# Attention followed by a Mish MLP on one core: casting loads and TensorE transposes for the first two batches, and units of work spread anew

## The chip, the cores and the metric

One NeuronCore of a Trainium2 chip runs the whole program. The metric is device time in microseconds (us) of one execution, as the median of several (tail_first_b has one run); a profile of one execution comes with it.

## The reference, cut to what matters

```python
q, k, v: (8 batches, 12 heads, 448 rows, 64) fp32
scores = q @ k.T / 8 ;  e = exp(scores - m)
attn   = e / (sum(e) + exp(-m))            # "softmax off by one"
x      = (attn @ v), heads side by side    # 3584 x 768
h      = x @ w_in                          # 768 -> 2048
g      = h * tanh(softplus(h))             # Mish
out    = g @ w_out                         # 2048 -> 768, fp32
```

The kernel leaves out m (the inputs are small), so the denominator is sum(e) + 1.

## The kernel before: the parts that matter

The program is a hand-written order of **slots**. Slot j (0 to 47) does the attention scores of head pair j; six slots make a batch, two slots make a **group** of four heads. At every even slot the sums and the product with v (attend) of the group before are done. Between them, TensorE gets **units** of the MLP of earlier batches: `mm1` (six matmuls of 448 columns, x by w_in, evicted by VectorE into `h_sb`) and `mm2` (eight matmuls of 384 columns, Mish(h) by w_out; two units make one output tile). Mish itself runs on ScalarE, which also does all exps; its table is exchanged before and after (1.28 us each time in the trace).

```python
    def load(j, names="kqv"):                      # fp32, 229 KB each, sync queue
        ...
            nc.sync.dma_start(out=st, in_=src[b, h0 : h0 + 2].rearrange("h (p t) d -> p h (t d)", t=NT))

    def do_cast(j, eng):                           # to bf16, on VectorE or Pool
        mb = half.tile([P, 2, NT, 2, D], BF16, tag="mb", name="mb")
        for i, name in enumerate("kq"):
            eng.tensor_copy(...)
        if j >= NPAIR:                             # batch 1 and later: DMA transpose
            qk = qk_pool.tile([128, 2, S], BF16, tag="qk", name="qk")
            nc.sync.dma_start_transpose(...)
            qk_t[j] = qk
        else:                                      # batch 0: TensorE, in transposes(j)
            cast[j] = mb

    def mish(b):
        ...
        for i in range(4):
            f = slice(i * n, (i + 1) * n)
            nc.scalar.activation(out=gm[:, f, :], in_=h_sb[:, f, 0:MAIN], func=AF.Mish)
        nc.scalar.activation(out=gt[:, :, o : o + TAIL], in_=h_sb[:, :, MAIN:S], func=AF.Mish)
        nc.scalar.preload_act_table_set("natural_log_exp_and_others")

        def slot(j, units, late=False):
            ...                                    # casts for j + 2, loads for j + 4
            scores(j, 0)
            take(1)                                # one unit
            if j + 1 < J: transposes(j + 1)
            if g is not None: sums(g)
            take(1)
            scores(j, 1)
            take((rest + 1) // 2)
            if g is not None: attend(g, 0); attend(g, 1)
            take(len(units), last=True)

        for p in range(B):
            m1 = mm1_units(p - 1) if p >= 1 else []
            m2 = mm2_units(p - 2) if p >= 2 else []   # 12 for even batches, 16 for odd ones
            for i in range(NPAIR):
                ...   # i = 0: four of m2; i = 1..4: four of m1 each; i = 5: what is left of m2
                if i == 4 and p >= 1:
                    mish(p - 1)                       # then eight of m2 at once
```

Of PSUM, the memory that matmuls write to, the kernel gives four banks to scores, two to attend, and two (pool `m`) to sums, transposes, `mm1` and `mm2` together.

The softmax here doesn't subtract the row's maximum and nothing guards it: scores larger than these inputs give would overflow.

Of the kernel before, what the change touches and what calls it, by code (L numbers as in the profile page):

```python
# [9 lines left out]
BF16 = mybir.dt.bfloat16  # L10
# [5 lines left out]
def kernel(  # L16
# [14 lines left out]
    nc = tc.nc  # L31

    B, H, S, D = q.shape
    d_model, d_ff = moe_w_in.shape
    NPAIR = H // 2
    J = B * NPAIR
    NT = 4
# [7 lines left out]
    FF_T = d_ff // 128  # L45
    HALF = d_model // 2
    SCALE = 1.0 / float(D) ** 0.5
    AHEAD = 4

    singles = ctx.enter_context(tc.tile_pool(name="singles", bufs=1))  # L50
    stage = ctx.enter_context(tc.tile_pool(name="stage", bufs=AHEAD - 1))
    half = ctx.enter_context(tc.tile_pool(name="half", bufs=3))
    v_pool = ctx.enter_context(tc.tile_pool(name="v", bufs=6))
    qk_pool = ctx.enter_context(tc.tile_pool(name="qk", bufs=4))
    e_pool = ctx.enter_context(tc.tile_pool(name="e", bufs=3))
    work = ctx.enter_context(tc.tile_pool(name="work", bufs=2))
# [9 lines left out]
    w_out_sb = singles.tile([128, FF_T, d_model], BF16, name="w_out_sb")  # L66
    h_sb = singles.tile([128, FF_T, S], FP32, name="h_sb")

    loaded, cast, qk_t, v_t, e_t, x_t = {}, {}, {}, {}, {}, {}
    rc_t, gm_t, gt_t = {}, {}, {}  # L70

    def load(j, names="kqv"):
        b, h0 = j // NPAIR, 2 * (j % NPAIR)
        for name in names:
            src = {"q": q, "k": k, "v": v}[name]
            st = stage.tile([P, 2, NT * D], FP32, tag=name, name=f"{name}_f")
            nc.sync.dma_start(  # L77
                out=st, in_=src[b, h0 : h0 + 2].rearrange("h (p t) d -> p h (t d)", t=NT)
            )
            loaded[j, name] = st  # L80

    def do_cast(j, eng):

        mb = half.tile([P, 2, NT, 2, D], BF16, tag="mb", name="mb")
        for i, name in enumerate("kq"):
            eng.tensor_copy(  # L86
                out=mb[:, i].rearrange("p t h d -> p h t d"),
                in_=loaded.pop((j, name)).rearrange("p h (t d) -> p h t d", d=D),
            )
        if j >= NPAIR:  # L90
            qk = qk_pool.tile([128, 2, S], BF16, tag="qk", name="qk")
            nc.sync.dma_start_transpose(
                out=qk.rearrange("c i (t p) -> c (i t) p", p=P),
                in_=mb.rearrange("p i t h d -> p (i t h d)"),
            )
            qk_t[j] = qk
        else:
            cast[j] = mb

    def cast_v(j):  # L100
        vb = v_pool.tile([P, 2, NT, D], BF16, tag="v", name="v_b")
        nc.gpsimd.tensor_copy(out=vb.rearrange("p h t d -> p h (t d)"), in_=loaded.pop((j, "v")))  # L102
        v_t[j] = vb

    def transposes(j):
        if j >= NPAIR:
            return
        mb = cast.pop(j)
        ps = m_pool.tile([128, 2, S], BF16, tag="m", name="tr_ps")
        for i in range(2):  # L110
            for t in range(NT):
                nc.tensor.transpose(
                    ps[:, i, t * P : (t + 1) * P],
                    mb[:, i, t].rearrange("p h d -> p (h d)"),
                    ident[0:P, 0:P],
                )
        qk = qk_pool.tile([128, 2, S], BF16, tag="qk", name="qk")
        nc.vector.tensor_copy(out=qk, in_=ps)
        qk_t[j] = qk
# [22 lines left out]
    def side_by_side(ps, g, weights):  # L142

        for t in range(NT):
            for c in range(4):
                nc.tensor.matmul(  # L146
                    ps[c * 32 : c * 32 + 32, 0:S],
                    lhsT=weights(2 * g + c // 2, c % 2, t),
                    rhs=e_t[2 * g + c // 2][:, t, c % 2, :],
                    start=(t == 0),  # L150
                    stop=(t == NT - 1),
                )

    def sums(g):
        den = m_pool.tile([128, 512], FP32, tag="m", name="den_ps")
        side_by_side(den, g, lambda j, h, t: ones[0:P, :])
        rc = work.tile([128, S], FP32, tag="rc", name="rc")
        nc.scalar.activation(out=rc, in_=den[:, 0:S], func=AF.Ln, bias=1.0)  # L158
        nc.scalar.activation(out=rc, in_=rc, func=AF.Exp, scale=-1.0)  # L159
        rc_t[g] = rc  # L160

    def attend(g, s):
        b, gi = divmod(g, GRP)
        if gi == 0 and s == 0:
            x_t[b] = work.tile([128, GRP, 2, S], BF16, tag="xT", name="xT")
        av = x_pool.tile([128, 512], FP32, tag="x", name="av_ps")
        side_by_side(
            av, g, lambda j, h, t: v_t[j][:, h, t, :].rearrange("p (d s) -> p s d", s=2)[:, s, :]
        )
        nc.vector.tensor_mul(x_t[b][:, gi, s, :], av[:, 0:S], rc_t[g])  # L170
        if s == 1:
            for j in (2 * g, 2 * g + 1):
                e_t.pop(j), v_t.pop(j)
            rc_t.pop(g)

    def mm1(b, ff, direct):
# [73 lines left out]
    def mm2_units(b):  # L250
        return [
            lambda t=t, n=n, part=part: mm2(b, t, n, part)
            for t in range(NC + b % 2)
            for n in range(2)
            for part in range(2)
        ]

    with tc.manual_schedule():
        nc.scalar.preload_act_table_set("natural_log_exp_and_others")
        load(0)  # L260
        load(1)
        load(2)
        make_identity(nc, ident)
        do_cast(0, nc.vector)
        cast_v(0)
        transposes(0)
        load(3)
        do_cast(1, nc.vector)
        cast_v(1)

        def load_w_in(i):
            c = slice(i * d_ff // 4, (i + 1) * d_ff // 4)
            for s in range(2):
                nc.gpsimd.dma_start(
                    out=w_in_sb[:, :, s, c],
                    in_=moe_w_in[:, c].rearrange("(g p s) f -> s p g f", p=128, s=2)[s],
                )

        def load_w_out(i):
            n = FF_T // 4  # L280
            nc.gpsimd.dma_start(
                out=w_out_sb[:, i * n : (i + 1) * n, :],
                in_=moe_w_out[i * n * 128 : (i + 1) * n * 128, :].rearrange(
                    "(f p) c -> p f c", p=128
                ),
            )

        def slot(j, units, late=False):




            def take(n, last=False):
                if late and not last:
                    return
                for _ in range(min(n, len(units))):
                    units.pop(0)()

            g = j // 2 - 1 if j % 2 == 0 and j >= 2 else None
            if j + 2 < J:  # L300
                do_cast(j + 2, nc.vector if j + 2 < NPAIR else nc.gpsimd)
                cast_v(j + 2)
            if j + AHEAD < J:
                load(j + AHEAD)
            if j <= 3:
                load_w_in(j)
            if 5 <= j <= 8:
                load_w_out(j - 5)
            rest = max(0, len(units) - 2)
            if j < J:  # L310
                scores(j, 0)
            take(1)
            if j + 1 < J:
                transposes(j + 1)
            if g is not None:
                sums(g)
            take(1)
            if j < J:
                scores(j, 1)
            take((rest + 1) // 2)  # L320
            if g is not None:
                attend(g, 0)
                attend(g, 1)
            take(len(units), last=True)

        for p in range(B):
            m1 = mm1_units(p - 1) if p >= 1 else []
            m2 = mm2_units(p - 2) if p >= 2 else []
            for i in range(NPAIR):
                late = p == 1 and i == 0  # L330
                if late:
                    units, m1 = m1[:2], m1[2:]
                elif i == 0:
                    units, m2 = m2[:4], m2[4:]
                elif i < 5:
                    units, m1 = m1[:4], m1[4:]
                else:
                    units, m2 = m2, []
                slot(p * NPAIR + i, units, late)
                if i == 4 and p >= 1:  # L340
                    mish(p - 1)
                    first, m2 = m2[:8], m2[8:]
                    for u in first:
                        u()
        m2 = mm2_units(B - 2)
        slot(J, m2[:4])
        m2 = m2[4:]
        m1 = mm1_units(B - 1, direct=True)
        while m1 or m2:
            if m1:  # L350
                m1.pop(0)()
            if m2 and len(m2) >= len(m1):
                m2.pop(0)()
        for u in mm2_units(B - 1):
            u()


# [28 lines left out]
```

## Time and profile before

| | before |
|---|---|
| median time | 479.41 us (3 runs, 479.09 to 489.27) |
| profiled execution | span 476.4 us, mean granted clock 0.965 |
| TensorE (PE) busy | 434.7 us, 91% |
| 16 DMA engines, 0 to 83 us | 8 or 9 tenths busy |

First, lines of the profile page's picture of the span in 40 slices of 11.9 us each. A digit is the busy share in tenths; PEclk is the granted TensorE clock in tenths. PE is TensorE, ACT ScalarE, DVE VectorE, POOL the engine GpSimd (Pool in the text), and L129 is line 129 of the kernel.

```profile
PE   3967697399998999999998999999998999999995
ACT  3873257935776559455766659455765658343200
PEclk9987799589999999999999999999999999999998
DMA  8999999419217860569117950579117600210222
```

From the ninth slice on PE is nearly full: mostly its work counts there. In the first eight slices PE is often not full, the clock dips, and DMA is at 8 or 9 in all but the last of them. So there are two stages with different limits, and one mean over the span would hide that.

Second, the chain of work that ended last, from its start (start us, us, what):

```profile
4.18 6.41 DMA q_f<-in_q_dram
10.65 7.00 DMA k_f<-in_k_dram
17.72 11.94 DMA v_f<-in_v_dram
29.66 22.01 DMA qk<-mb
...
52.71 4.47 PE h_ps L179 x12
...
57.70 2.38 PE h_ps L179 x12
...
81.63 5.60 ACT gm L207 x4
```

The start hangs on loads and on one DMA transpose that took 22 us to land. Twelve matmuls of `mm1` take 4.47 us right after that wait, and the next twelve 2.38 us, five us later.

Third, the waits of PE in the timeline (start us, us, engine, line, what; in brackets the idle time before, and what ended it):

```profile
36.76 0.99 PE L129 MATMUL s_ps<-qk 64*112 64x448 bf16 x4 [3.64 <-DMA qk<-mb]
51.71 0.99 PE L129 MATMUL s_ps<-qk 64*112 64x448 bf16 x4 [5.94 <-DMA qk<-mb]
90.45 0.62 PE L129 MATMUL s_ps<-qk 64*112 64x448 bf16 x2 [9.57 <-ACT e L136]
```

The last one is Mish of batch 0: ScalarE is busy with it from 80.3 to 89.5 us, and TensorE's next scores need an exp to free their PSUM buffer.

Fourth, from the steady part, again the chain of waits:

```profile
143.55 3.35 ACT e L136 x4
...
249.86 3.35 ACT e L136 x4
...
356.18 3.35 ACT e L136 x4
```

Once in two batches the slot after Mish has no units left, and PE waits for exps.

### The profile page before, as it was taken

What the parts mean: (1) busy time and instruction counts of PE and PEld (TensorE: products, weight loads), DVE (VectorE), ACT (ScalarE), POOL (GpSimd) and SP (SyncE); (2) the same over time, 40 slices, a digit from 0 to 9 for tenths busy, and PEclk for the clock granted to TensorE, in tenths of its full rate; (3) what the DMA queues carried; (4) which work ended last, traced back from release to release, by engine and by line L of the source; (5) the groups of instructions that cost most, each with busy time, mean ns of one, the idle gap of its engine ahead of it and who ended that gap; (6) DMA issues with size and microseconds to landing.
All of it is one profiled execution on the core that took longest, in us unless ns stands there. A gap on an engine that the chain in (4) does not pass through costs nothing.

```text
span 476.4 us, 7816 instructions
## 1 busy us (share of the span) xinstructions
PE 434.7 (91%) x3248; PEld 205.3 (43%) x3248; DVE 140.6 (30%) x235; ACT 266.9 (56%) x323; POOL 90.6 (19%) x150
## 2 busy tenths in 40 slices
PE   3967697399998999999998999999998999999995
PEld 1422243144453445544453445544453445555563
DVE  3512143024321343134421343134421343110021
ACT  3873257935776559455766659455765658343200
POOL 1722234203102140024103230114103100000000
PEclk9987799589999999999999999999999999999998
DMA  8999999419217860569117950579117600210222
GB/s 220 252 217 202 201 222 247 131 34 240 70 34 187 170 174 0 144 156 258 41 35 189 220 124 8 141 168 239 44 35 187 150 1 27 61 48 1 66 67 67
DMA packets 83364, 60.48 MB, mean 127 GB/s; under 512 B 42368, under 2 KB 79744, under 8 KB 83328
## 3 DMA queue, kind: packets, MB, share of 16 engines
q1 hardware_dynamic: 78016, 53.69, 48.1%
q0 software_dynamic: 5312, 6.29, 8.0%
q8 instruction: 25, 0.41, 0.4%
q14 instruction: 11, 0.09, 0.1%
HBM read 45.61 MB, written 11.01 MB: 119 GB/s over the span
## 4 chain that ended last, share of the span: by engine, by line
PE 83%; DMA 10%; ACT 5%; SPq 1%; issue 0%; DVE 0%
PE h_ps L179 32%; PE o_ps L231 32%; PE s_ps L129 8%; PE av_ps L146 7%; DMA qk<-mb 5%; PE den_ps L146 4%; ACT e L136 3%; DMA v_f<-in_v_dram 3%; DMA k_f<-in_k_dram 1%; DMA q_f<-in_q_dram 1%; ACT gm L207 1%; SPq L77 1%; ACT L209 0%; ACT L207 0%; ACT gt L208 0%
## 5 line engine op out<-in xcount | busy, mean ns | idle before, releaser
L136 ACT ACTIVATE e<-s_ps 112x896 bf16<-112x896 f32 x192 | 164.2, 916 | 137.2 <-PE s_ps L129 137.1
L179 PE MATMUL h_ps<-xT,w_in_sb 128*128 128x448 bf16 x768 | 163.3, 357 | 0.0
L231 PE MATMUL o_ps<-w_out_sb,gm 128*128 128x384 bf16 x768 | 133.3, 328 | 0.0
L179 PEld LDWEIGHTS <-w_in_sb 128*128 128x128 bf16 x768 | 68.9, 98 | 85.5 <-issue 31.9
L187 DVE COPY h_sb<-h_ps 128x448 f32<-128x448 f32 x112 | 70.0, 625 | 114.9 <-PE h_ps L179 114.9
L231 PEld LDWEIGHTS <-gm 128*128 128x128 bf16 x768 | 73.4, 98 | 57.0 <-issue 10.3
L129 PE MATMUL s_ps<-qk 64*112 64x448 bf16 x384 | 64.0, 398 | 31.5 <-ACT e L136 19.5
L239 DVE COPY o_sb<-o_ps 128x384 f32<-128x384 f32 x56 | 31.2, 558 | 162.9 <-PE o_ps L231 155.6
L86 POOL CAST mb<-k_f 112x512 bf16<-112x512 f32 x42 | 25.9, 617 | 184.3 <-DMA k_f<-in_k_dram 159.7
L129 PEld LDWEIGHTS <-qk 64*112 64x112 bf16 x384 | 20.2, 131 | 70.1 <-issue 55.8
L102 POOL CAST v_b<-v_f 112x512 bf16<-112x512 f32 x48 | 29.6, 616 | 88.0 <-PE av_ps L146 62.6
L146 PE MATMUL av_ps<-e,v_b 112*32 112x448 bf16 x768 | 42.9, 367 | 0.0
L170 DVE TENSOR_TENSOR xT<-av_ps,rc 128x448 bf16<-128x448 f32 x48 | 30.0, 625 | 40.3 <-PE av_ps L146 38.3
L207 ACT ACTIVATE gm<-h_sb 128x1536 bf16<-128x1536 f32 x28 | 39.2, 1471 | 0.1
L86 POOL CAST mb<-q_f 112x512 bf16<-112x512 f32 x42 | 25.9, 616 | 13.6 <-DMA q_f<-in_q_dram 13.0
L146 PEld LDWEIGHTS <-v_b 112*32 112x32 bf16 x768 | 18.9, 99 | 22.3 <-issue 9.1
L158 ACT ACTIVATE rc<-den_ps 128x448 f32<-128x448 f32 x24 | 13.1, 544 | 22.5 <-PE den_ps L146 22.5
L146 PE MATMUL den_ps<-e,ones 112*32 112x448 bf16 x384 | 25.3, 388 | 0.0
L231 PE MATMUL o_ps<-w_out_sb,gt 128*128 128x384 bf16 x128 | 22.0, 326 | 0.0
L191 ACT ACTIVATE gm<-h_ps 128x384 bf16<-128x384 f32 x16 | 7.9, 491 | 22.7 <-PE h_ps L179 22.7
L231 PEld LDWEIGHTS <-gt 128*128 128x128 bf16 x128 | 12.0, 98 | 9.5 <-issue 2.0
L159 ACT ACTIVATE rc<-rc 128x448 f32<-128x448 f32 x24 | 13.8, 576 | 0.8
(21 smaller groups left out, 68.6 us busy)
## 6 DMA issues: line engine op xcount, KB each, us to landing
k_f<-in_k_dram SPq DMA_DIRECT2D x48, 224.0 KB, 4.1
q_f<-in_q_dram SPq DMA_DIRECT2D x48, 224.0 KB, 4.3
v_f<-in_v_dram SPq DMA_DIRECT2D x48, 224.0 KB, 4.5
w_in_sb<-in_moe_w_in_dram POOLq DMA_DIRECT2D x8, 384.0 KB, 16.1
w_out_sb<-in_moe_w_out_dram POOLq DMA_DIRECT2D x4, 768.0 KB, 12.8
out_dram<-o_sb SPq DMA_DIRECT2D x8, 336.0 KB, 3.1
out_dram<-o_sb SPq DMA_DIRECT2D x8, 288.0 KB, 2.7
out_dram<-o_sb SPq DMA_DIRECT2D x8, 240.0 KB, 2.6
```

The source lines that it names most:

```text
L86: eng.tensor_copy(out=mb[:, i].rearrange("p t h d -> p h t d"), in_=loaded.pop((j, name)).rearrange("p h (t d) -> p h t d", d=D),)
L102: nc.gpsimd.tensor_copy(out=vb.rearrange("p h t d -> p h (t d)"), in_=loaded.pop((j, "v")))
L129: nc.tensor.matmul(sp[0:P, h, 0:S], lhsT=qk[r, 0, t * P : (t + 1) * P], rhs=qk[r, 1, :], start=True, stop=True,)
L136: nc.scalar.activation(out=e_t[j][:, t], in_=sp[0:P, :, 0:S], func=AF.Exp, scale=SCALE)
L146: nc.tensor.matmul(ps[c * 32 : c * 32 + 32, 0:S], lhsT=weights(2 * g + c // 2, c % 2, t), rhs=e_t[2 * g + c // 2][:, t, c % 2, :], start=( ...
L159: nc.scalar.activation(out=rc, in_=rc, func=AF.Exp, scale=-1.0)
L170: nc.vector.tensor_mul(x_t[b][:, gi, s, :], av[:, 0:S], rc_t[g])
L179: nc.tensor.matmul(hp[:, 0:S], lhsT=w_in_sb[:, dm // 2, dm % 2, ff * 128 : (ff + 1) * 128], rhs=x_t[b][:, dm // 2, dm % 2, :], start=(dm = ...
L187: nc.vector.tensor_copy(out=h_sb[:, ff, :], in_=hp[:, 0:S])
L207: nc.scalar.activation(out=gm[:, f, :], in_=h_sb[:, f, 0:MAIN], func=AF.Mish)
L231: nc.tensor.matmul(op[:, 0:HALF], lhsT=lhs, rhs=w_out_sb[:, ff, n * HALF : (n + 1) * HALF], start=(ff == 0), stop=(ff == FF_T - 1),)
L239: nc.vector.tensor_copy(out=o_sb[:, n * HALF : (n + 1) * HALF], in_=op[:, 0:HALF])
```

## The change

Its intent: bring q, k and v of batches 0 and 1 in as bf16 straight away, by DMAs that cast (issued by Pool, one ring, fixed order, w_in in between); transpose them on TensorE, so that no DMA transpose runs among the first loads; fetch w_out behind them; run Mish of batch 0 one slot later, where units of batch 1 can run beside it; and spread the units so that the slot after Mish always has some. The core of the diff, with cuts:

```diff
-    AHEAD = 4
+    SW = 2 * NPAIR
+    def load_cast(g, names="kqv", pairs=((0, 4),)):
+        kq, vb = group_tiles(g)
+        ...
+                nc.gpsimd.dma_start(out=dst, in_=rows_of(src, b, 4 * gi + h, n))
     def transposes(j):
-        if j >= NPAIR:
+        if j >= SW:
             return
+                for h in range(2):          # two half-width transposes in place of one
+                    nc.tensor.transpose(ps[h * D : h * D + D, i, t * P : (t + 1) * P], kq[:, i, o + h, t], ident[0:P, 0:P])
+    fetch = {
+        0: [lambda: load_w_in(3)],
+        3: [lambda: load_cast(3), lambda: load_w_out(0)],
+        5: [lambda: load_cast(4), lambda: load_w_out(1)],
+        7: [lambda: load_cast(5), lambda: load_w_out(2), lambda: load_w_out(3)],
+    }
+    def slot(j, units, pre=0, mish_of=None):
+        ...                                 # fetch, casts for j + 2 and loads for j + 4 from slot 12 on
+        run(units, pre)
+        if g is not None: sums(g)
+        if mish_of is not None: mish(mish_of)
+        scores(j, 0)
+        if g is not None: attend(g, 0); attend(g, 1)
+        run(units, (len(units) + 1) // 2)
+        if j + 1 < J: transposes(j + 1)
+        scores(j, 1)
+        run(units)
     with tc.manual_schedule():
+        load_cast(0, "kq", ((0, 2),))
+        load_cast(0, "v")
+        load_cast(0, "kq", ((2, 2),))
+        load_cast(1, "kq")
+        load_w_in(0)
+        load_cast(1, "v")
+        load_w_in(1)
+        load_cast(2)
+        load_w_in(2)
         ...
+                elif p == 1:
+                    slot(j, cut(m1, (2, 3, 3, 3, 3, 2)[i]))
+                elif p == 2:
+                    if i == 0:
+                        slot(j, cut(m1, 6), mish_of=0)
+                    elif i < 5:
+                        slot(j, [m1.pop(0)] + cut(m2, 1) + cut(m1, 2 if i < 3 else 1), pre=1)
+                    else:
+                        slot(j, m2, pre=1)
+                elif i == 0:
+                    slot(j, cut(m2, len(m2) - 10 + p % 2 * -2), pre=1)
+                elif i < 5:
+                    slot(j, cut(m1, 4), pre=1)
+                else:
+                    slot(j, m2, pre=1)
+                if i == 4 and p >= 2:
+                    mish(p - 1)
+                    run(cut(m2, len(m2) * 2 // 3))
```

From slot 12 on (batch 2 and later) loads, Pool casts and DMA transposes stay as they were.

More of the change, by code (lines that the diff above doesn't have):

```diff
@@ L47 @@
     SCALE = 1.0 / float(D) ** 0.5
-    AHEAD = 4
+    SW = 2 * NPAIR
     singles = ctx.enter_context(tc.tile_pool(name="singles", bufs=1))
-    stage = ctx.enter_context(tc.tile_pool(name="stage", bufs=AHEAD - 1))
+    stage = ctx.enter_context(tc.tile_pool(name="stage", bufs=3))
     half = ctx.enter_context(tc.tile_pool(name="half", bufs=3))
-    v_pool = ctx.enter_context(tc.tile_pool(name="v", bufs=6))
+    v_pool = ctx.enter_context(tc.tile_pool(name="v", bufs=3))
     qk_pool = ctx.enter_context(tc.tile_pool(name="qk", bufs=4))
@@ L67, with rows_of, group_tiles, load @@
     h_sb = singles.tile([128, FF_T, S], FP32, name="h_sb")
-    loaded, cast, qk_t, v_t, e_t, x_t = {}, {}, {}, {}, {}, {}
+    loaded, kq_t, qk_t, v_t, e_t, x_t = {}, {}, {}, {}, {}, {}
     rc_t, gm_t, gt_t = {}, {}, {}
-    def load(j, names="kqv"):
+    def rows_of(src, b, h0, n):
+        return src[b, h0 : h0 + n].rearrange("h (p t) d -> p h (t d)", t=NT)
+    def group_tiles(g):
+        if g not in kq_t:
+            kq_t[g] = half.tile([P, 4, 2, NT * D], BF16, tag="kq", name="kq")
+            v_t[g] = v_pool.tile([P, 4, NT * D], BF16, tag="v", name="v_b")
+        return kq_t[g], v_t[g]
+    def load_cast(g, names="kqv", pairs=((0, 4),)):
+        kq, vb = group_tiles(g)
+        b, gi = divmod(g, GRP)
+        for h, n in pairs:
+            for name in names:
+                if name == "v":
+                    dst, src = vb[:, h : h + n], v
+                else:
+                    i = "kq".index(name)
+                    dst = kq.rearrange("p (i hh) two c -> p i (hh two) c", i=2)[:, i, h : h + n]
+                    src = (k, q)[i]
+                nc.gpsimd.dma_start(out=dst, in_=rows_of(src, b, 4 * gi + h, n))
+    def load(j):
         b, h0 = j // NPAIR, 2 * (j % NPAIR)
-        for name in names:
-            src = {"q": q, "k": k, "v": v}[name]
+        for name, src in (("k", k), ("q", q), ("v", v)):
             st = stage.tile([P, 2, NT * D], FP32, tag=name, name=f"{name}_f")
-            nc.sync.dma_start(
-                out=st, in_=src[b, h0 : h0 + 2].rearrange("h (p t) d -> p h (t d)", t=NT)
-            )
+            nc.sync.dma_start(out=st, in_=rows_of(src, b, h0, 2))
             loaded[j, name] = st
-    def do_cast(j, eng):
-        mb = half.tile([P, 2, NT, 2, D], BF16, tag="mb", name="mb")
+    def do_cast(j):
+        kq, vb = group_tiles(j // 2)
+        o = 2 * (j % 2)
+        mb = kq[:, o : o + 2].rearrange("p i hh (t h d) -> p i (hh t) h d", h=2, d=D)
         for i, name in enumerate("kq"):
-            eng.tensor_copy(
+            nc.gpsimd.tensor_copy(
                 out=mb[:, i].rearrange("p t h d -> p h t d"),
@@ L89, in do_cast @@
             )
-        if j >= NPAIR:
-            qk = qk_pool.tile([128, 2, S], BF16, tag="qk", name="qk")
-            nc.sync.dma_start_transpose(
-                out=qk.rearrange("c i (t p) -> c (i t) p", p=P),
-                in_=mb.rearrange("p i t h d -> p (i t h d)"),
-            )
-            qk_t[j] = qk
-        else:
-            cast[j] = mb
-    def cast_v(j):
-        vb = v_pool.tile([P, 2, NT, D], BF16, tag="v", name="v_b")
-        nc.gpsimd.tensor_copy(out=vb.rearrange("p h t d -> p h (t d)"), in_=loaded.pop((j, "v")))
-        v_t[j] = vb
+        nc.gpsimd.tensor_copy(out=vb[:, o : o + 2], in_=loaded.pop((j, "v")))
+        qk = qk_pool.tile([128, 2, S], BF16, tag="qk", name="qk")
+        nc.sync.dma_start_transpose(
+            out=qk.rearrange("c i (t p) -> c (i t) p", p=P),
+            in_=mb.rearrange("p i t h d -> p (i t h d)"),
+        )
+        qk_t[j] = qk
     def transposes(j):
-        if j >= NPAIR:
+        if j >= SW:
             return
-        mb = cast.pop(j)
+        o = 2 * (j % 2)
+        kq = kq_t[j // 2].rearrange("p (i hh) two (t d) -> p i (hh two) t d", i=2, d=D)
         ps = m_pool.tile([128, 2, S], BF16, tag="m", name="tr_ps")
@@ L111, in transposes @@
             for t in range(NT):
-                nc.tensor.transpose(
-                    ps[:, i, t * P : (t + 1) * P],
-                    mb[:, i, t].rearrange("p h d -> p (h d)"),
-                    ident[0:P, 0:P],
-                )
+                for h in range(2):
+                    nc.tensor.transpose(
+                        ps[h * D : h * D + D, i, t * P : (t + 1) * P],
+                        kq[:, i, o + h, t],
+                        ident[0:P, 0:P],
+                    )
         qk = qk_pool.tile([128, 2, S], BF16, tag="qk", name="qk")
@@ L147, in side_by_side @@
                     ps[c * 32 : c * 32 + 32, 0:S],
-                    lhsT=weights(2 * g + c // 2, c % 2, t),
+                    lhsT=weights(c, t),
                     rhs=e_t[2 * g + c // 2][:, t, c % 2, :],
@@ L155, in sums @@
         den = m_pool.tile([128, 512], FP32, tag="m", name="den_ps")
-        side_by_side(den, g, lambda j, h, t: ones[0:P, :])
+        side_by_side(den, g, lambda c, t: ones[0:P, :])
         rc = work.tile([128, S], FP32, tag="rc", name="rc")
@@ L167, in attend @@
         side_by_side(
-            av, g, lambda j, h, t: v_t[j][:, h, t, :].rearrange("p (d s) -> p s d", s=2)[:, s, :]
+            av,
+            g,
+            lambda c, t: v_t[g].rearrange("p c (t d s) -> p c t s d", s=2, d=D // 2)[:, c, t, s],
         )
@@ L171, in attend @@
         if s == 1:
-            for j in (2 * g, 2 * g + 1):
-                e_t.pop(j), v_t.pop(j)
+            e_t.pop(2 * g), e_t.pop(2 * g + 1), v_t.pop(g)
             rc_t.pop(g)
@@ L256, in mm2_units, with load_w_in, load_w_out @@
         ]
+    def load_w_in(i):
+        c = slice(i * d_ff // 4, (i + 1) * d_ff // 4)
+        for s in range(2):
+            nc.gpsimd.dma_start(
+                out=w_in_sb[:, :, s, c],
+                in_=moe_w_in[:, c].rearrange("(g p s) f -> s p g f", p=128, s=2)[s],
+            )
+    def load_w_out(i):
+        n = FF_T // 4
+        nc.gpsimd.dma_start(
+            out=w_out_sb[:, i * n : (i + 1) * n, :],
+            in_=moe_w_out[i * n * 128 : (i + 1) * n * 128, :].rearrange("(f p) c -> p f c", p=128),
+        )
@@ new lines, with run @@
+    fetch = {
[4 more added lines that the diff above has]
+    }
+    def run(units, n=None):
+        for _ in range(len(units) if n is None else min(n, len(units))):
+            units.pop(0)()
+    def slot(j, units, pre=0, mish_of=None):
+        for f in fetch.get(j, ()):
+            f()
+        if SW <= j + 2 < J:
+            do_cast(j + 2)
+        if SW <= j + 4 < J:
+            load(j + 4)
+        run(units, pre)
+        g = j // 2 - 1 if j % 2 == 0 and j >= 2 else None
+        if g is not None:
+            sums(g)
+        if mish_of is not None:
+            mish(mish_of)
+        if j < J:
+            scores(j, 0)
+        if g is not None:
+            attend(g, 0)
+            attend(g, 1)
+        run(units, (len(units) + 1) // 2)
+        if j + 1 < J:
+            transposes(j + 1)
+        if j < J:
+            scores(j, 1)
+        run(units)
@@ L258, with cut @@
+    def cut(m, n):
+        part = m[:n]
+        del m[:n]
+        return part
     with tc.manual_schedule():
         nc.scalar.preload_act_table_set("natural_log_exp_and_others")
-        load(0)
-        load(1)
-        load(2)
+        load_cast(0, "kq", ((0, 2),))
         make_identity(nc, ident)
-        do_cast(0, nc.vector)
-        cast_v(0)
-        transposes(0)
-        load(3)
-        do_cast(1, nc.vector)
-        cast_v(1)
-        def load_w_in(i):
-            c = slice(i * d_ff // 4, (i + 1) * d_ff // 4)
-            for s in range(2):
-                nc.gpsimd.dma_start(
-                    out=w_in_sb[:, :, s, c],
-                    in_=moe_w_in[:, c].rearrange("(g p s) f -> s p g f", p=128, s=2)[s],
-                )
@@ L279, in load_w_out @@
-        def load_w_out(i):
-            n = FF_T // 4
-            nc.gpsimd.dma_start(
-                out=w_out_sb[:, i * n : (i + 1) * n, :],
-                in_=moe_w_out[i * n * 128 : (i + 1) * n * 128, :].rearrange(
-                    "(f p) c -> p f c", p=128
-                ),
-            )
-        def slot(j, units, late=False):
-            def take(n, last=False):
-                if late and not last:
-                    return
-                for _ in range(min(n, len(units))):
-                    units.pop(0)()
-            g = j // 2 - 1 if j % 2 == 0 and j >= 2 else None
-            if j + 2 < J:
-                do_cast(j + 2, nc.vector if j + 2 < NPAIR else nc.gpsimd)
-                cast_v(j + 2)
-            if j + AHEAD < J:
-                load(j + AHEAD)
-            if j <= 3:
-                load_w_in(j)
-            if 5 <= j <= 8:
-                load_w_out(j - 5)
-            rest = max(0, len(units) - 2)
-            if j < J:
-                scores(j, 0)
-            take(1)
-            if j + 1 < J:
-                transposes(j + 1)
-            if g is not None:
-                sums(g)
-            take(1)
-            if j < J:
-                scores(j, 1)
-            take((rest + 1) // 2)
-            if g is not None:
-                attend(g, 0)
-                attend(g, 1)
-            take(len(units), last=True)
@@ L329 @@
             for i in range(NPAIR):
-                late = p == 1 and i == 0
-                if late:
-                    units, m1 = m1[:2], m1[2:]
+                j = p * NPAIR + i
+                if p == 0:
+                    slot(j, [])
+                elif p == 1:
[7 more added lines that the diff above has]
+                        slot(j, m2, pre=1)
                 elif i == 0:
-                    units, m2 = m2[:4], m2[4:]
+                    slot(j, cut(m2, len(m2) - 10 + p % 2 * -2), pre=1)
                 elif i < 5:
-                    units, m1 = m1[:4], m1[4:]
+                    slot(j, cut(m1, 4), pre=1)
                 else:
-                    units, m2 = m2, []
-                slot(p * NPAIR + i, units, late)
-                if i == 4 and p >= 1:
+                    slot(j, m2, pre=1)
+                if i == 4 and p >= 2:
                     mish(p - 1)
-                    first, m2 = m2[:8], m2[8:]
-                    for u in first:
-                        u()
+                    run(cut(m2, len(m2) * 2 // 3))
         m2 = mm2_units(B - 2)
-        slot(J, m2[:4])
-        m2 = m2[4:]
+        slot(J, cut(m2, 4), pre=2)
         m1 = mm1_units(B - 1, direct=True)
@@ L353 @@
                 m2.pop(0)()
-        for u in mm2_units(B - 1):
-            u()
+        run(mm2_units(B - 1))
 _INS = ['q', 'k', 'v', 'moe_w_in', 'moe_w_out']
```

## The prediction

> **What bounds it now.** From about 100 us on it is TensorE. The busy table by stretches has PE busy 60.0 of 60 us in 180 to 240 and 57.95 of 60 in 240 to 300; the chain of waits is 83% PE. One batch costs 51.8 or 54.6 us by turns (distances of the chain's 10.40 us blocks of output matmuls). The longer ones stall: in the slot after Mish no TensorE unit is left and the scores wait for exps (the chain's "ACT e" pieces of 3.35 us at 143.6, 249.9, 356.2).
>
> The first 100 us are bound by DMA: 16 engines at 111 to 123% share from 10 to 80 us, and the chain there is q_f 6.4, k_f 7.0, v_f 11.9 and the DMA transpose 22.0 us. PE waited 3.6 and 5.9 us for two DMA transposes of batch 1, then 9.6 us for ScalarE (Mish of batch 0). Each long wait also slows the clock: 12 matmuls took 4.47 us instead of 2.38 after the second. The Trainium skill, "TensorE: Matmul & The Clock Gate", "HAM oscillation", says so of idle gaps over about 3.4 us; the granted clock of 0.61 to 0.71 between 80 and 100 us agrees.
>
> **What changes.** Casting DMAs must come from GpSimd (the skill, "DMA: Bandwidth & Descriptors", "SWDGE vs HWDGE vs iDMA"); in the trace w_in does. Gone: six early DMA transposes (229 KB each, 4.0 us median but up to 22), 12 DVE casts (0.43) and Pool casts (0.62). Added: 96 small transposes more (I estimate 0.5 to 0.8 us a pair, against 0.57 for the eight before) and six DVE copies (0.62). But all loads now queue in one ring in a fixed order, with w_in ahead of group 3, and the fp32 loads of pairs 12 to 14 (2.06 MB) wait for nothing and go out at 1 us, beside the first group.
>
> **Costs.** Packets: 60 ns per 1 KB plain, about 95 ns per 2 KB read of w_in, 131 to 145 per 3 KB of w_out. I estimate 47 to 60 ns for a casting 1 KB row. Before k/q of group 3 land, 13.4 MB must be read: at 300 to 345 GB/s that is 42 to 47 us, and slot 6 starts only then. Slot 7 will start near 53 to 55 against 51.7. Slots 6 to 11 are then PE bound (8.0 us even, 5.7 odd). Mish of batch 0 is half hidden (about 5 us of wait instead of 9.6), but the half-finished output tiles of slots 13 to 16 hold one of two PSUM buffers: about four waits of 0.8 us on DVE evacuations. The start is about even: +4 to -5, centre -1 us.
>
> Steady state: units left for the slot after Mish remove about 2.8 us in each of p = 4 and 6 and at p = 3's start: about -7 us with fewer mode changes.
>
> **Predicted: 471.5 us, 80% range 461 to 481.** Faster by over 2%: 0.40; within 2%: 0.57; slower by over 2%: 0.03.
>
> **Signs.** Right: no DMA transpose in the first 50 us; PE waits for group 2 and 3 loads near 30 and 43 us; slot 12 starts at 83 to 90; a shorter ACT wait there; no 3.35 us "ACT e" pieces after 200 us; distance of two batches 103.5 instead of 106.3. Wrong if: casting rows reach well over 350 GB/s (start gains 5 to 8 us, total near 464), or fall under 280 (no gain at all), or the GpSimd ring leaves bubbles, or TensorE waits for buffers in slots 13 to 16 more than I count.

## The result and the profile after

| | before | after |
|---|---|---|
| median time | 479.25 us (4 runs) | 460.94 us (4 runs, 460.36 to 462.87) |
| ratio of fast runs | | 0.964 (95%: 0.959 to 0.969) |
| profiled span, granted clock | 476.4 us, 0.965 | 458.6 us, 0.989 |
| end of slot 18, equal work done | 155.9 us | 145.9 us |
| from there to the end | 320.5 us | 312.7 us |

A ratio here is the mean time of one kernel's fast runs over that of the other's fast runs of the same rounds, so it is not quite the ratio of the medians quoted beside it. Some runs of before are "slow" (485 to 497 us); they are left out of the ratios and not explained. All outputs are right.

The change gains 18 us: 10.0 us by the end of slot 18, 7.8 us after it. The time falls just below the forecast's range, whose lower end was 461.

The same lines of the page (a slice is now 11.5 us):

```profile
PE   1877999589889999999999999999999999999995
ACT  2767667936595559466685559465675559342200
PEclk9979999899999999999999999999999999999999
DMA  9999997153145931695056941795057501210122
```

PE is at 9 from the fifth slice on, but for slices 8, 9, 11 and 12. DMA is at 9 for six slices (69 us), where it was at 8 or 9 for seven (83 us) before. The clock still dips twice, but less: to 7 in the third slice and to 8 in the eighth, where it was at 7 in slices 4 and 5 and at 5 in the eighth before.

The busy time by stretches (PE, PEld, DVE, ACT, POOL with counts; then granted clock, DMA share, and GB/s) shows the new ring at work:

```profile
10.00:20.00 10.00, 8.29 (x76) 3.48 (x76) 1.25 (x2) 7.41 (x10) 5.51 (x8) 1.00 1.33 202
20.00:30.00 10.00, 7.44 (x94) 3.33 (x88) 2.40 (x4) 7.19 (x9) 4.07 (x6) 0.77 1.32 203
30.00:40.00 10.00, 7.39 (x95) 3.12 (x95) 2.40 (x4) 7.63 (x10) 4.28 (x6) 0.89 1.29 204
40.00:50.00 10.00, 9.72 (x104) 4.64 (x105) 4.22 (x8) 6.35 (x9) 3.36 (x5) 1.00 1.32 201
```

The last column counts what is written: this queue's whole 10.42 MB in the page is the bf16 size of w_in, w_out and two batches of q, k and v. The sources are fp32, so 203 GB/s written is, worked out, about 406 GB/s read, steady over 40 us whatever the mix of 1, 2 and 3 KB rows. The clock of 0.77 in the second line is looked at under "The skill" below.

The chain from the start:

```profile
3.28 7.56 DMA v_b<-in_v_dram
...
11.86 12.82 DMA w_in_sb<-in_moe_w_in_dram
...
25.99 11.65 DMA kq<-in_q_dram
...
37.69 0.39 PE tr_ps L129 x8
...
43.97 0.51 PE tr_ps L129 x16
```

It hangs on loads until group 3's q lands at 37.7 us, and on TensorE after that. Sixteen transposes take 0.51 us once warm.

The waits of PE that are left:

```profile
86.86 2.40 PE L197 MATMUL h_ps<-xT,w_in_sb 128*128 128x448 bf16 x6 [5.25 <-DVE h_sb L205]
...
98.66 1.29 PE L197 MATMUL h_ps<-xT,w_in_sb 128*128 128x448 bf16 x6 [0.20 <-DVE h_sb L205]
100.67 1.30 PE L197 MATMUL h_ps<-xT,w_in_sb 128*128 128x448 bf16 x6 [0.71 <-DVE h_sb L205]
102.68 0.94 PE L163 MATMUL den_ps<-e,ones 112*32 112x448 bf16 x16 [0.71 <-DVE h_sb L205]
...
115.69 1.30 PE L197 MATMUL h_ps<-xT,w_in_sb 128*128 128x448 bf16 x6 [0.71 <-DVE h_sb L205]
117.70 0.94 PE L163 MATMUL den_ps<-e,ones 112*32 112x448 bf16 x16 [0.71 <-DVE h_sb L205]
```

The 5.25 us are Mish of batch 0, the others are the half-finished output tiles. In the steady part the chain after 140 us has only these pieces of ScalarE:

```profile
197.06 1.73 ACT e L153 x2
...
299.97 1.74 ACT e L153 x2
```

### The profile page after: what moved, and what is told of

Same layout as the page of the kernel before. It is cut to its first block, busy times and chain, and to the rows that moved or that the text cites. A ratio compares the mean times of both kernels' runs of the same rounds, so it can differ in the third digit from the quotient of the medians.

```text
span 458.6 us, 7956 instructions
## 1 busy us (share of the span) xinstructions
PE 428.5 (93%) x3392; PEld 209.7 (46%) x3392; DVE 137.9 (30%) x229; ACT 265.7 (58%) x323; POOL 89.2 (19%) x146
## 3 DMA queue, kind: packets, MB, share of 16 engines
q0 software_dynamic: 13696, 10.42, 14.6%
## 4 chain that ended last, share of the span: by engine, by line
PE 83%; DMA 7%; ACT 7%; DVE 1%; issue 1%; POOL 1%; POOLq 0%
PE h_ps L197 31%; PE o_ps L249 30%; PE s_ps L146 9%; PE av_ps L163 7%; PE den_ps L163 4%; ACT e L153 3%; DMA w_in_sb<-in_moe_w_in_dram 3%; DMA kq<-in_q_dram 3%; ACT gm L225 2%; DMA v_b<-in_v_dram 2%; DVE h_sb L205 1%; PE tr_ps L129 1%; ACT L225 1%; POOL kq L93 0%; ACT gt L226 0%
## 5 line engine op out<-in xcount | busy, mean ns | idle before, releaser
L197 PE MATMUL h_ps<-xT,w_in_sb 128*128 128x448 bf16 x768 | 159.6, 355 | 6.9 <-DVE h_sb L205 6.9
L249 PE MATMUL o_ps<-w_out_sb,gm 128*128 128x384 bf16 x768 | 131.0, 326 | 0.0
L197 PEld LDWEIGHTS <-w_in_sb 128*128 128x128 bf16 x768 | 70.5, 98 | 86.5 <-issue 28.6
L146 PE MATMUL s_ps<-qk 64*112 64x448 bf16 x384 | 61.2, 388 | 5.4 <-ACT e L153 4.4
L108 POOL CAST kq<-k_f 112x512 bf16<-112x512 f32 x36 | 22.2, 617 | 190.0 <-DMA k_f<-in_k_dram 179.7
L163 PE MATMUL av_ps<-e,v_b 112*32 112x448 bf16 x768 | 41.4, 358 | 0.0
L112 POOL CAST v_b<-v_f 112x512 bf16<-112x512 f32 x36 | 22.2, 616 | 54.0 <-PE av_ps L163 48.4
L108 POOL CAST kq<-q_f 112x512 bf16<-112x512 f32 x36 | 22.2, 617 | 5.5 <-DMA q_f<-in_q_dram 4.0
L129 PE MATMUL tr_ps<-ident,kq 112*64 112x112 bf16 x192 | 9.3, 244 | 11.1 <-DMA kq<-in_k_dram 9.0
L163 PEld LDWEIGHTS <-ones 112*32 112x32 bf16 x384 | 8.9, 98 | 17.3 <-issue 13.8
```

The costliest lines, as they stand in the source:

```text
L108: nc.gpsimd.tensor_copy(out=mb[:, i].rearrange("p t h d -> p h t d"), in_=loaded.pop((j, name)).rearrange("p h (t d) -> p h t d", d=D),)
L112: nc.gpsimd.tensor_copy(out=vb[:, o : o + 2], in_=loaded.pop((j, "v")))
L129: nc.tensor.transpose(ps[h * D : h * D + D, i, t * P : (t + 1) * P], kq[:, i, o + h, t], ident[0:P, 0:P],)
L146: nc.tensor.matmul(sp[0:P, h, 0:S], lhsT=qk[r, 0, t * P : (t + 1) * P], rhs=qk[r, 1, :], start=True, stop=True,)
L163: nc.tensor.matmul(ps[c * 32 : c * 32 + 32, 0:S], lhsT=weights(c, t), rhs=e_t[2 * g + c // 2][:, t, c % 2, :], start=(t == 0), stop=(t == ...
L197: nc.tensor.matmul(hp[:, 0:S], lhsT=w_in_sb[:, dm // 2, dm % 2, ff * 128 : (ff + 1) * 128], rhs=x_t[b][:, dm // 2, dm % 2, :], start=(dm = ...
```

## The experiments

Unless a diff says otherwise, it is against the changed kernel. Times are medians; "before" stands for the runs of before in the same rounds. What a part costs is given as a difference of medians from the changed kernel, in part across chips. By the ratios to before the four runs of the first chip come out 2 to 3 us lower, as before was slower there (see the ranges), so a single cost is known to some 2 to 3 us. The record's verdict against before is "faster" for tail_first, best2 and best3 and "unclear" for the others that have a ratio; their 95% intervals are within about 0.008 of the ratio.

### Taking the parts away: a_old_steady, b1_old, b1_fp32_petr, mish_old

These four shared a chip (before: fast runs 477.8 to 482.7 us).

**a_old_steady** keeps the new start and puts the old slot order and shares back from batch 3 on (core of the diff; `slot_old` is the slot of before):

```diff
                 elif i == 0:
-                    slot(j, cut(m2, len(m2) - 10 + p % 2 * -2), pre=1)
+                    slot_old(j, cut(m2, 4))
                 elif i < 5:
-                    slot(j, cut(m1, 4), pre=1)
+                    slot_old(j, cut(m1, 4))
                 else:
-                    slot(j, m2, pre=1)
+                    slot_old(j, cut(m2, len(m2)))
-                    run(cut(m2, len(m2) * 2 // 3))
+                    run(cut(m2, 8 if p > 2 else len(m2) * 2 // 3))
```

> The changed kernel, but from batch 3 on with the slot order and the shares of units of before. Reading of the two traces: at equal work done (end of the slot with index 18) the changed kernel is 10.0 us ahead (145.9 against 155.9 us) and gains 7.8 more until the end. If the gains are separate, this one loses the 7.8: about 468.7 us, ratio to before 0.978. Rival: the later gain is a consequence of the start (loads that come earlier), then it stays near 461.

Measured: 470.86 us, ratio 0.980: it loses 9.9 us by the medians and 7.4 us by the ratios. The later gain belongs to the spread, not to the start. Its chain shows the old pieces again:

```profile
242.85 3.35 ACT e L153 x4
...
349.16 3.35 ACT e L153 x4
```

**b1_old** brings batch 1 in as before:

```diff
-    SW = 2 * NPAIR
+    SW = NPAIR
-        3: [lambda: load_cast(3), lambda: load_w_out(0)],
-        5: [lambda: load_cast(4), lambda: load_w_out(1)],
-        7: [lambda: load_cast(5), lambda: load_w_out(2), lambda: load_w_out(3)],
+        3: [lambda: load_w_out(0)],
+        5: [lambda: load_w_out(1)],
+        7: [lambda: load_w_out(2), lambda: load_w_out(3)],
```

> Batch 1 is loaded as before (fp32 on the sync queue, cast on Pool, DMA transposes); all else as changed. Theory 1 (the start's 10 us come from the way batch 1 is brought in): 8 to 12 us slower than the changed kernel, 469 to 473 us, with waits of TensorE for DMA transposes between 30 and 60 us. Theory 2 (they come from Mish of batch 0 one slot later): 461 to 463.

Measured: 465.47 us, ratio 0.969. That lies between the two theories: about 4 us of the 10 (4.5 by the medians, 2.6 by the ratios) hang on batch 1's way in. The list of waits of the first 110 us names them (in total us, times, longest); it is of its slowest run, 469.15 us, and the trace that is kept, of another run, has 6.0, 3 and 3.0:

```profile
PE s_ps L146 <- DMA qk<-kq: 8.4, 3, 3.6
```

**b1_fp32_petr** loads batch 1 as b1_old does, but transposes it on TensorE (core of the diff against b1_old):

```diff
+        if j < 2 * NPAIR:
+            return                     # in do_cast: no DMA transpose for batch 1
-        if j >= SW:
+        if j >= 2 * NPAIR:             # in transposes(j)
             return
+                if j >= SW:
+                    nc.tensor.transpose(ps[:, i, t * P : (t + 1) * P], mb[:, i, t], ident[0:P, 0:P])
+                    continue
```

> Batch 1 loaded in fp32 on the sync queue and cast on Pool, but transposed on TensorE; no early DMA transposes. Theory 1a (the casting ring, which read 406 GB/s alone, is what wins): the fp32 rows share the engines, reading falls to 330 to 350 GB/s and groups 3 to 5 come 4 to 7 us later: 464 to 468 us. Theory 1b (only the absence of the six early DMA transposes matters): 461 to 463.

Measured: 460.61 us, ratio 0.958; no slower than the changed kernel. So theory 1a falls: for batch 1 the cast on the way in brings nothing, and what cost b1_old its 4 us (4.9 against this run, on the same chip) are the six DMA transposes. A likely reason, argued and not shown: the bytes read before group 3 is complete are the same. In the changed kernel the 2.06 MB that the sync queue loads at once are pairs 12 to 14, which nobody needs yet; here they are pairs 6 to 8. In its trace TensorE reaches group 3 at 37.26 us without a wait.

**mish_old** puts Mish of batch 0 back:

```diff
-                    slot(j, cut(m1, (2, 3, 3, 3, 3, 2)[i]))
+                    slot(j, cut(m1, (2, 4, 4, 4, 2, 0)[i]))
-                        slot(j, cut(m1, 6), mish_of=0)
+                        slot(j, cut(m1, 6))
+                if i == 4 and p == 1:
+                    mish(0)
```

> The changed kernel with Mish of batch 0 back after slot 10, its 16 units in slots 6 to 10 and none in slot 11. Theory 1: it loses only the difference of the two waits (9.6 us before, 5.3 us after): about 465 us, +3 to +5. Theory 2 (Mish's place is the start's gain): +9 to +10, about 471 us.

Measured: 466.85 us, ratio 0.971: 5.9 us by the medians, a little over theory 1's top, and 3.5 by the ratios, inside it. The old wait is back, longer than the new one by 4.4 us, and the matmuls after it run at half clock (granted clock 0.50 until 93 us):

```profile
86.21 0.62 PE L146 MATMUL s_ps<-qk 64*112 64x448 bf16 x2 [9.69 <-ACT e L153]
```

### The other side of it: after_again, ring12, dump_ring, b_new_steady

These four shared another chip (before: fast runs 476.1 to 480.1 us). **after_again** is the changed kernel itself.

> The changed kernel unedited, so that it shares this chip and these runs of before with the next three: ratio 0.964 as on the first chip.

Measured: 461.75 us, ratio 0.966.

**b_new_steady** is before with only the new steady part: from p = 3 on its loop calls the new `slot`, with the shares of the new `elif` branches shown in the change.

> The kernel before with only the new slot order and shares of units from batch 3 on. If the gains of start and steady part are separate: 7 to 9 us faster than before, ratio 0.981 to 0.985. If the new spread pays only together with the new start: within 1%.

Measured: one fast run of 468.24 us, and three slow ones (480.3 to 489.2), so no ratio could be given. The fast run is 8 to 12 us below the fast runs of before, near the expectation; alone it shows little, but a_old_steady says the same from the other side.

**ring12** takes the early fp32 loads off the sync queue:

```diff
-            nc.sync.dma_start(out=st, in_=rows_of(src, b, h0, 2))
+            eng = nc.gpsimd if j < SW + 3 else nc.sync
+            eng.dma_start(out=st, in_=rows_of(src, b, h0, 2))
```

> The changed kernel with the fp32 loads of pairs 12 to 14 (2.06 MB) issued from Pool in program order, so that they no longer run beside the first group. If the landing of the casting loads gates the start one to one, group 0 lands 2 to 3 us earlier, group 3's k/q near 33 us instead of 36.5 and 37.7, and the total falls by 3 to 4 us. If ScalarE's exps (about 4 us a slot) have become the gate by then, 1 us or less.

Measured: 460.19 us, ratio 0.963, about 1.5 us less. The expectation missed. Group 0 came 3 us earlier (first transposes at 4.36 us against 7.40 in after_again), but group 3's q only 1.0 us earlier (36.07 against 37.09). Alone, the ring read only about 270 GB/s from 3 to 9 us; the 2.06 MB beside it had partly run in time that the ring left free.

**dump_ring** is ring12 with 2.75 MB of fp32 loads without a cast at the head of the ring:

```diff
+        dump = h_sb.rearrange("p f s -> p (f s)")
+        for i in range(6):
+            nc.gpsimd.dma_start(
+                out=dump[0:P, i * 1024 : (i + 1) * 1024].rearrange("p (h c) -> p h c", h=4),
+                in_=rows_of(v, 2 + i, 0, 4),
+            )
         load_cast(0, "kq", ((0, 2),))
```

> The kernel ring12 with six extra fp32 loads without a cast (2.75 MB, result unused) at the head of the Pool ring. Their rate tells what makes the ring fast. If it is the ring (packets of the software ring overlap), they read near 400 GB/s: 6.9 us for them. If it is the cast (half the bytes written), they read 260 to 340 GB/s as plain loads on the sync queue do: 8 to 10.5 us. Either way everything behind them comes later by that much, which is as large as the error of my landing time for group 3 (42 to 47 us forecast, 37.7 measured): if that error is what the forecast missed, the total rises by 6 to 9 us over ring12; if the start isn't gated by these loads, by under 3.

Measured: 467.76 us, ratio 0.979: 7.6 us over ring12, 6.0 over after_again. Two stretches of its DMA view, 3 to 9 us (plain rows) and 13 to 19 us (casting rows), both on the same ring and both reading 1 KB rows of fp32. They differ in more than the cast: the plain rows go out as packets of 3.7 KB on average, the casting ones as packets of 0.5 KB. The columns of the queue's line are packets, MB written, and share of 16 engines.

```profile
DMA packets 435, 1.59 MB, mean 264 GB/s; under 512 B 48, under 2 KB 48, under 8 KB 435
...
q0 software_dynamic: 435, 1.59, 97.6%
```

```profile
DMA packets 2308, 1.16 MB, mean 193 GB/s; under 512 B 114, under 2 KB 2300, under 8 KB 2308
...
q0 software_dynamic: 2308, 1.16, 141.4%
```

Plain rows: 264 GB/s read and written. Casting rows: 193 written, so 386 read. So the ring alone does not make rows fast: on it plain rows do no better than on the sync queue of before (261 GB/s from 4 to 10 us). That the cast alone does it is not shown. In ring12 casting rows on the same ring, in the same 3 to 9 us, read only 270 GB/s:

```profile
DMA packets 1663, 0.81 MB, mean 135 GB/s; under 512 B 81, under 2 KB 1663, under 8 KB 1663
...
q0 software_dynamic: 1663, 0.81, 111.8%
```

What else it takes (time since the ring's start, loads queued ahead, the size of packets) was not separated. And with group 3's q at 43.2 us instead of 36.1, the time rises by as much, 7.6 us for 7.2: the start is gated by the landing of the ring's loads nearly one to one, and group 3's landing is now where the forecast had put it. All groups come later here, group 0 by 10 us, so it is not group 3's landing alone that was tested.

### Do the parts add up: b1_mish_old

This and the next three shared a third chip (before: fast runs 476.2 to 479.8 us). The edit is b1_old's and mish_old's together.

> Both undone: batch 1 loaded and transposed as before and Mish of batch 0 at its old place; batch 0 still comes by casting DMAs. Alone they cost 4.5 and 6 us. Theory: they add up to the start's whole 10 us and the casting loads of batch 0 bring nothing (attend of group 2 starts at 40.2 us before and 41.0 after): 470 to 473 us, ratio to before 0.980 to 0.987. Rival: the casting loads of batch 0 carry a part of the start's gain: under 469.

Measured: 468.82 us, ratio 0.983. The median missed the range in us, the ratio lies in it. Both together cost about 7.5 us against the changed kernel (8 to 9 by the ratios); alone they cost 4.5 and 5.9 (2.6 and 3.5 by the ratios). Whether they add up is not decided by that. With the steady part's 7.4 to 9.9 us this nearly makes up the 18, so little (about 1 to 3 us) is left for the casting loads of batch 0, the new order inside the first slots and all else; none of these was taken away alone.

### The waits that were left: pairs, tail_first, tail_units

**pairs** puts both halves of an output tile into one slot:

```diff
-                        slot(j, [m1.pop(0)] + cut(m2, 1) + cut(m1, 2 if i < 3 else 1), pre=1)
+                        slot(j, cut(m1, 1) + cut(m2, 2 * (i % 2)) + cut(m1, 1 if i % 2 else 2), pre=1)
```

> The changed kernel with both halves of an output tile of batch 0 in the same slot (two in slots 13 and 15, none in 14 and 16), so that no half-finished tile holds a PSUM buffer while weight matmuls and sums want it. The trace shows four waits of 0.71 us on DVE and one of 0.2 in slots 13 to 16. If that is what they cost: 2 to 3 us faster, about 459. If the waits only move: within 0.5 us of the changed kernel.

Measured: 458.45 us, ratio 0.960: 2.5 to 3.3 us less. Of TensorE's waits for VectorE to empty a PSUM buffer only the one of Mish is left:

```profile
PE h_ps L197 <- DVE h_sb L205: 5.3, 1, 5.3
```

**tail_first** runs Mish of the tail columns ahead of the four main parts. The tail part reads every row of `h_sb`, so no copy of batch 1 could enter `h_sb` before it was done (in the changed kernel's trace one such copy waits 6.3 us for it):

```diff
+        nc.scalar.activation(out=gt[:, :, o : o + TAIL], in_=h_sb[:, :, MAIN:S], func=AF.Mish)
         for i in range(4):
             f = slice(i * n, (i + 1) * n)
             nc.scalar.activation(out=gm[:, f, :], in_=h_sb[:, f, 0:MAIN], func=AF.Mish)
-        nc.scalar.activation(out=gt[:, :, o : o + TAIL], in_=h_sb[:, :, MAIN:S], func=AF.Mish)
```

> The changed kernel with Mish of the tail columns ahead of the four main parts. The trace has TensorE wait 5.25 us in slot 12 for a DVE copy into h_sb, which itself waits for the tail's Mish, the last reader of every row of h_sb. If that is the cause, the copy is free after the tail and the first main part (1.0 + 1.4 us) instead of after all five, the 5.25 us go but for what the exps then hold, and the total falls by 3 to 5 us, to about 457. Rival, as in my forecast: the wait is for the scores' buffers, which the exps free after Mish; then under 1 us.

Measured: 462.82 us, ratio 0.969: no gain. One of its four executions took 1484.86 us, and its profile fell on that one (see the last section), so a single look was taken again as **tail_first_b**:

> tail_first again, for its profile: about 462.5 us. If both waits stand one behind the other, TensorE waits about 1 us for the copy into h_sb and about 4 us for an exp before the second half of the scores of slot 12, in place of the one wait of 5.25 us.

Measured: 463.84 us (one run, so its state is unknown). Its waits in slot 12:

```profile
84.72 1.29 PE L197 MATMUL h_ps<-xT,w_in_sb 128*128 128x448 bf16 x6 [1.14 <-DVE h_sb L205]
90.41 0.62 PE L146 MATMUL s_ps<-qk 64*112 64x448 bf16 x2 [4.39 <-ACT e L153]
```

The 5.25 us have become 1.14 and 4.39: two waits stand one behind the other, and TensorE sits before the scores while three units that nothing holds stand behind them in the program. **tail_units** moves these:

```diff
-        run(units, (len(units) + 1) // 2)
+        run(units, None if mish_of is not None else (len(units) + 1) // 2)
```

> tail_first, and in slot 12 all six weight-matmul units ahead of the second half of the scores (three of them stood behind it). If the two waits stand one behind the other, the freed units now fill the second: 3 to 5 us faster than the changed kernel, 456 to 458. If something else holds slot 12: within 1 us of it.

Measured, on a fourth chip (before: median 478.22 us): 457.79 us, ratio 0.958. The wait for the scores is 0.99 us now:

```profile
84.28 4.70 PE L197 MATMUL h_ps<-xT,w_in_sb 128*128 128x448 bf16 x24 [1.13 <-DVE h_sb L205]
89.97 0.40 PE L146 MATMUL s_ps<-qk 64*112 64x448 bf16 x2 [0.99 <-ACT e L153]
```

### Together: best2 and best3

**best2** is ring12, pairs and tail_first with two moves in the ring; **best3** adds tail_units' move.

```diff
-        0: [lambda: load_w_in(3)],
-        3: [lambda: load_cast(3), lambda: load_w_out(0)],
+        3: [lambda: load_cast(3), lambda: load_w_in(3), lambda: load_w_out(0)],
-        load_cast(0, "v")
         load_cast(0, "kq", ((2, 2),))
+        load_cast(0, "v")
```

> Together: ring12, pairs, tail_first, the second pair's k/q ahead of v in the ring, and the last quarter of w_in behind group 3. If the parts add (1.5, 2.5 and 4 us) and the reordered ring brings 2 us: 450 to 453 us, ratio to before 0.940 to 0.946. If one hides another: 454 to 457.

Measured: 455.65 us, ratio 0.953 (third chip): in the range for the case that one part hides another, which tail_first_b's trace explains.

> best2 with the same move: 451 to 453 us if the gain of tail_units adds, ratio to before 0.943 to 0.948.

Measured: 449.16 us (6 runs, 448.42 to 449.99), ratio 0.940 (fourth chip), a little better than expected and 6% faster than before. In its trace TensorE no longer waits for group 3.

## Why the prediction was wrong

The forecast was 471.5 us (461 to 481); measured were 460.94. The direction and most mechanisms were right. Its sum had two terms:

| term | forecast | measured |
|---|---|---|
| start | -1 us (+4 to -5) | -10.0 us |
| steady part | about -7 us | -7.8 us in the traces; a_old_steady +7.4 (ratios) to +9.9 (medians) |

**The step that failed is the size of the casting loads' rate.** The forecast said "13.4 MB must be read: at 300 to 345 GB/s that is 42 to 47 us, and slot 6 starts only then". The ring read about 406 GB/s, and group 3's k and q were there at 36.5 and 37.7 us. The estimate of "47 to 60 ns for a casting 1 KB row" was itself right: in dump_ring 2308 packets took 141.4% of 16 engines' time for 6 us, which is 59 ns each. What it missed is the overlap. If each of 16 engines handles one row at a time, 47 to 60 ns give 273 to 349 GB/s, the forecast's span and a little below; but the rows overlapped, so that an engine finished one every 42 ns (386 GB/s). In the trace of before plain rows moved 261 GB/s at 102% share, and no stretch that was looked at had a long run of casting rows with nothing beside it. dump_ring also shows what the term is worth: with the landing back at 43.2 us, inside the forecast's span, the time is 467.76 us, inside its range. So 6 to 7.6 us of the 10.5 us error is this term. The forecast had named the case ("casting rows reach well over 350 GB/s", start gains 5 to 8 us, total near 464), but gave it too little room. What the other 3 to 4.5 us are was not isolated. The transposes took 0.51 us per pair once warm, the low end of the estimate (they are 144 more, 3392 matmuls against 3248 on the pages, where the forecast counted 96), and the granted clock was 0.989 instead of 0.965.

**Where the start's gain came from.** Not from the cast itself for batch 1 (b1_fp32_petr: no loss without it). Taken away one by one, the DMA transposes of batch 1 cost 3 to 5 us and Mish's place 3.5 to 6; together 7.5 to 9. The forecast expected the new order of loads, with w_in ahead of group 3, to give this back. At the measured rate it did not; dump_ring, with the landing that the forecast expected, gave back 6 to 7.6 us.

**Mish of batch 0**: "about 5 us of wait instead of 9.6" held as a number: 5.25. The reason did not, so this was partly luck: the forecast's sign was "a shorter ACT wait there", but TensorE waited for VectorE's copy into `h_sb`, which Mish was still reading, and the wait for the scores' buffers stands hidden behind it (4.39 us in tail_first_b).

**Half-finished tiles**: "about four waits of 0.8 us" held: four of 0.71 and one of 0.20. pairs takes them away and gains about what they sum to, 3.0 us.

**Steady part**: "no 3.35 us pieces after 200 us" held (one of 1.74 us), and two batches take 102.9 us (the chain's blocks of output matmuls at 174.12, 277.04 and 379.95) against 103.5 forecast and 106.3 before.

**Slots**: slot 7's scores began at 46.2 us ("53 to 55"), slot 12 at 76.1 ("83 to 90"); both at least 7 us before the forecast's spans, the loads' error handed on. The waits for groups 2 and 3 came at 25.5 and 37.7 us instead of "near 30 and 43". No DMA transpose was issued before 50.5 us, as forecast.

**The skill.** Its page "TensorE: Matmul & The Clock Gate", "HAM oscillation", warns of idle gaps over about 3.4 us. The long gaps here agree: twelve matmuls took 4.47 us behind a gap of 5.94 us and 2.38 otherwise, and in the changed kernel six took 2.40 us behind 5.25 and 1.24 otherwise. But a long gap is not the only way to a slow clock: in the changed kernel the granted clock was 0.50 from 26 to 32 us, and the longest gap in the ten us before that was 1.02 us (PE was busy 40% of the time from 23 to 25 us).

## What to carry to other kernels

A forecast that lets a load gate the start stands or falls with that load's rate: take the rate from a stretch in which the same kind of row (same length, same cast) runs alone, late enough after the start (270 GB/s from 3 to 9 us in ring12, 386 from 13 to 19 us in dump_ring), and where the trace has none, widen the range on that side. Before blaming or praising a part of a change for the whole, take each part away alone; here the part that looked like the point of the change (the cast of batch 1) was worth nothing, and the absence of a few DMA transposes and a better place for one activation block were worth most of the start's gain. When a wait goes and the time does not, look for the next wait behind it, and for work that stands in order behind that.

## What the Trainium skill lacked or had wrong

- "DMA: Bandwidth & Descriptors", "Where 436 GB/s comes from", says that for transfers between HBM and SBUF "the HBM side (~358) binds". With this program on one core, the casting ring read about 406 GB/s (203 written) for 40 us, so as a limit for one core alone that sentence is too low; the measurement decides. The same page, "SWDGE vs HWDGE vs iDMA", has one load stream alone at 408.7 GB/s with 4 KiB rows, which fits.
- The same page says, also under "SWDGE vs HWDGE vs iDMA", that a cast must come from GpSimd, but gives no rate for it. Measured on one ring, rows of 1 KB fp32: with a cast to bf16 270 GB/s read from 3 to 9 us (ring12) and 386 from 13 to 19 us (dump_ring), without a cast 264.
- The same page, "Latency and other measured facts", gives 261 GB/s for DMA transposes with a non-contiguous middle dimension. Here one of 229 KB landed after a median of 4.0 us (57 GB/s, with all that lies between issue and landing) and took up to 22 us among loads. An estimate of the rate itself: from 50 to 60 us of the changed kernel 882 packets of a transpose, 0.26 MB, took 19.9% of 16 engines' time, about 130 GB/s if they alone filled the engines.
- One of four executions of tail_first took 1484.86 us. TensorE was busy for 1465.9 of 1483.1 us, twelve matmuls took 8.7 us instead of 2.4, and the recorded granted clock was 1.00. The nearest is in "TensorE: Matmul & The Clock Gate", "Seeing it yourself": clock events that cannot be trusted, and a clock stuck at a quarter for over 50 us; no page has it for a whole execution. These twelve were 3.6 times slower, which is near a quarter of the clock, but it was seen once and stays unexplained.
